# The opening of a scan-and-gate kernel: gates by token tile, a second DMA queue, and moved statistics

## The chip, the cores and the metric

The kernel runs on one core of a Trainium2 chip. The metric is the device time of one execution in microseconds. The kernel before takes 182.96 us in the median of three runs (182.48 to 183.02). Engines are named as the profile names them: PE is TensorE (PEld its weight loads), DVE is VectorE, ACT is ScalarE, POOL is GpSimd, SP is SyncE, which here only issues DMAs.

## The reference, cut to what matters

The input `x` has 2048 tokens of 448 features (bf16). It is normalised over the features, and the normalised tokens feed two branches: a diagonal complex linear recurrence over time with 448 states, and a gated feed-forward product with 1792 hidden columns. The output is `x + s * silu(branch B)`.

```python
xn = _layernorm(x, axis=-1)                       # (x - mean) / sqrt(var + 1e-5)
# branch A: recurrence
dt = exp(log_dt); Lam_bar = exp(dt * Lam); B_bar = ((Lam_bar - 1) / Lam)[:, None] * Bmat
Bu = einsum("bld,pd->blp", xn + 0j, B_bar)
for t in range(L): h = Lam_bar[None, :] * h + Bu[:, t, :]
s = 2.0 * einsum("blp,dp->bld", hseq, Cmat).real + xn * Dskip
# branch B: gated product
g = xn @ w_gate; u = xn @ w_up; z = (sigmoid(g) * u) @ w_down
return x + s * silu(z)
```

## The kernel before, in words

The 2048 tokens are cut into four chunks of 512 columns, and each chunk into four token tiles of 128 rows. A chunk is normalised by token tile, turned so that features lie on partitions (`xnT`), multiplied with the gate and up weights (14 hidden tiles of 128, `ft` 0 to 13), and with B for the recurrence (`bu`, four state tiles); the recurrence is done by VectorE with sines, cosines and a scan instruction; later come the down products (`d_ps`) and the output products (`y_ps`). 448 features are three and a half times 128: a product with `wg` or `wu` has three whole blocks (`k` = 0, 1, 2) and a half block of 64 rows in `wt` (gate tail in the upper rows of the tile, up tail in the lower). From the hidden tiles 4 and 5 on, products run as pairs of 64-row halves side by side on PE (line 514). Every engine works in the order in which the kernel writes its instructions: `keep_order` (line 60) ties each to the one before it on its engine. In the steady part a planner (`at`, `rest`, `fill`, `queue`) places VectorE's pieces beside PE's groups; it starts with `emit_line(0, ((4, 5), (6, 7), (-1, 8), (-2, 9), (-3, 10), (11, 12), (-4, 13)))`, where a positive number is a hidden tile and a negative one a state tile.

The opening is everything before that line. It is written out by hand:

- SP issues x tile 0 (line 144), x tile 1 (145), x tiles 2 and 3 (149), the gate and up weights of columns 0 to 511 (line 150, six DMAs), those of columns 512 to 1279 (line 158), and x of chunk 1 (159). ACT issues the three rows of recurrence constants (line 142). After the opening SP issues four transposing loads of B (line 294), the weights from column 1280 (line 1025), the skip row and x of chunk 2.
- Statistics of chunk 0: tiles 0, 1 and 3 by `ln_stats` on DVE (lines 216 and 217) and `ln_inv` on ACT (a logarithm and an exponential, lines 249 and 250). Tile 2 by sums and squares on ACT (lines 224 to 231), and the power on POOL (line 244).
- Each tile is normalised on DVE (line 272), turned by four PE transposes (line 286) into one of two banks `tps`, and copied to `xnT` by DVE (`ln_out`, line 289).
- PE warms up on dummy products (`warm`, line 200), then does the gate products of hidden tiles 0 to 2 on the first 256 columns (token tiles 0 and 1; `gu_wholes`, line 713), the up products on them in two parts, with the transposes of tiles 2 and 3 between, then the half blocks (`gu_half`, line 706) on the lower and the upper 256 columns, and then the whole blocks on the upper columns and hidden tile 3.
- The sine tables need, for each of the four state tiles, the angle in whole turns (`emit_whole`, ACT, line 424, rounded by a conversion to integers), its fraction and absolute fraction (`emit_frac`, `emit_abs`, DVE, lines 429 and 435), a sine and a cosine (ACT, lines 440 and 443), and a negative (`emit_neg`, DVE, line 452); POOL mirrors them later (line 455). `emit_steps`, `emit_den` are small POOL operations.
- `gu_out` and `up_copy` (lines 719 and 1000) empty the banks of hidden tiles 0 to 3 by a tanh on ACT and a halving copy on DVE. PSUM has eight banks; the eight sums of hidden tiles 0 to 3 fill them, and the group (4, 5) takes the first four that come free.
- ACT's function tables: a logarithm and exponential set is loaded at line 929; a dummy Silu at line 962 brings in the set that also has sine and tanh; the sigmoid set follows with line 752.

Of the kernel before, what the change touches and what calls it, by code (L numbers as in the profile page):

```python
# [10 lines left out]
FP32 = mybir.dt.float32  # L11
BF16 = mybir.dt.bfloat16
I32 = mybir.dt.int32
ALU = mybir.AluOpType
ACT = mybir.ActivationFunctionType

S_TOK = 2048
D = 448
F = 1792
P = 128  # L20
TC = 512
HC = TC // 2
# [10 lines left out]
GATE_K, UP_K = (0, 2, 3), (0, 1, 3)  # L33
# [3 lines left out]
MAGIC = 12582912.0  # L37
CLAMP = 1.0 - 2e-6
LN_AND_EXP = 6
SIN_SCALE = TWO_PI * CLAMP  # L40


# [29 lines left out]
def kernel(  # L72
# [17 lines left out]
    nc = tc.nc  # L90
    pe, act, dve, pool, sync = nc.tensor, nc.scalar, nc.vector, nc.gpsimd, nc.sync
    w = ctx.enter_context(tc.tile_pool(name="w", bufs=1))
    cp = ctx.enter_context(tc.tile_pool(name="cp", bufs=2))
    sp = ctx.enter_context(tc.tile_pool(name="sp", bufs=2))
# [6 lines left out]
    x_src = A_x.rearrange("b (n p) d -> p (b n) d", p=P)  # L101


    x_t = [w.tile([P, TPC, D], BF16, name=f"x{c}", tag=f"x{c}") for c in range(3)]
# [3 lines left out]
    xnT = [w.tile([P, KT, TC], BF16, name=f"xnT{c}") for c in range(3)]  # L108
    xnT.append(xnT[0])

    wg = w.tile([P, 3, F], BF16, name="wg")
    wu = w.tile([P, 3, F], BF16, name="wu")
# [11 lines left out]
    def load_w(eng, f0, f1, tails_first=False):  # L124
        def rows(mat, r0, r1):
            m = mat[r0:r1, f0:f1]
            return m.rearrange("(kt p) f -> p kt f", p=P) if r1 - r0 > P else m

        eng.dma_start(out=wg[:, 1:3, f0:f1], in_=rows(B_w_gate, 192, 448))
        eng.dma_start(out=wg[:, 0, f0:f1], in_=rows(B_w_gate, 0, 128))  # L130
        up = ((wu[:, 0:2, f0:f1], rows(B_w_up, 0, 256)), (wu[:, 2, f0:f1], rows(B_w_up, 320, 448)))
        tails = ((wt[0:64, f0:f1], rows(B_w_gate, 128, 192)), (wt[64:128, f0:f1], rows(B_w_up, 256, 320)))
        for o, i in (tails + up if tails_first else up + tails):
            eng.dma_start(out=o, in_=i)
# [7 lines left out]
        eng.dma_start(out=rows[i:i + 1, :], in_=vec.rearrange("(o p) -> o p", o=1))  # L142

    sync.dma_start(out=x_t[0][:, 0, :], in_=x_src[:, 0, :])
    sync.dma_start(out=x_t[0][:, 1, :], in_=x_src[:, 1, :])
    load_row(act, 0, A_log_dt)
    load_row(act, 1, A_Lambda_im)
    load_row(act, 2, A_Lambda_re)
# [6 lines left out]
            x_t.append(w.tile([P, TPC, D], BF16, name="x3", tag="tc_re"))  # L155
        sync.dma_start(out=x_t[c][:], in_=x_src[:, c * TPC:(c + 1) * TPC, :])

    load_w(sync, 512, 1280, True)
    load_x(1)

    ctr = {}
# [16 lines left out]
    hpi = w.tile([P, 1], FP32, name="hpi")  # L178
# [13 lines left out]
    iota_f = sp.tile([P, HC], FP32, name="iota_f", tag="ctmp")  # L192
# [5 lines left out]
    def warm(n, t=ident):  # L198
        for _ in range(n):
            pe.matmul(warm_ps[:], lhsT=t[:, 0:P], rhs=t[:, 0:P], start=True, stop=True)  # L200
# [13 lines left out]
    def ln_stats(t):  # L214
        stats = cp.tile([P, 6], FP32, name="stats")
        dve.bn_stats(out=stats[:], in_=x_t[t // TPC][:, t % TPC, :])
        dve.bn_aggr(out=mv[:, t, :], in_=stats[:])


    sums = w.tile([P, NT, 2], FP32, name="sums")  # L220

    def ln_sum(t):
        c, j = divmod(t, TPC)
        act.activation(junk[:], x_t[c][:, j, :], ACT.Copy, accum_out=sums[:, t, 0:1])

    def ln_mean(t, n):
        act.activation(mv[:, t:t + n, 0:1], sums[:, t:t + n, 0:1], ACT.Copy, scale=1.0 / D)

    def ln_square(t):
        c, j = divmod(t, TPC)  # L230
        act.activation(junk[:], x_t[c][:, j, :], ACT.Square, bias=mv[:, t, 0:1], scale=-1.0,
                       accum_out=sums[:, t, 1:2])
# [15 lines left out]
    def ln_inv(t):  # L248
        act.activation(lnv[:, t, :], mv[:, t, 1:2], ACT.Ln, bias=epsb[:])
        act.activation(rsd[:, t, :], lnv[:, t, :], ACT.Exp, scale=-0.5)  # L250

    def ln_pow_of(t, n, var, scale):
        pool.tensor_scalar(out=ve[:, t:t + n, :], in0=var, scalar1=scale, scalar2=EPS, op0=ALU.mult, op1=ALU.add)
        ln_pow(t, n)
# [30 lines left out]
        for kt in range(KT):  # L285
            pe.transpose(tps[j % 2][:, kt, :], xb[:, j, K_ROWS[kt]:K_ROWS[kt] + P], ident[:])  # L286

    def ln_out(j):
        dve.tensor_copy(out=xnT[0][:, :, j * P:(j + 1) * P], in_=tps[j % 2][:])  # L289

# [14 lines left out]
    K = {}  # L307
# [35 lines left out]
    def emit_anf():  # L343
        dve.tensor_single_scalar(out=K["anf"][:].bitcast(I32), in_=K["nf"][:].bitcast(I32), scalar=0x7FFFFFFF,
                                 op=ALU.bitwise_and)

    def emit_step_sines():
        sn, cs, nf, anf = col("sn", 2 * KT), col("cs", 2 * KT), K["nf"], K["anf"]
        act.activation(sn[:], nf[:], ACT.Sin, scale=-SIN_SCALE)
        act.activation(cs[:], anf[:], ACT.Sin, scale=-TWO_PI, bias=hpi[:])  # L350
        K.update(sn=sn, cs=cs)
# [70 lines left out]
    def emit_whole(pt):  # L422
        whole = sp.tile([P, HC], I32, name="whole", tag=("ta", "tb", "tcs", "tb")[pt])
        act.activation(whole[:], iota_f[:], ACT.Copy, scale=K["turn"][:, pt:pt + 1])
        K[pt] = whole

    def emit_frac(pt):
        f = sp.tile([P, HC], FP32, name="frac", tag="wv")
        dve.scalar_tensor_tensor(out=f[:], in0=iota_f[:], scalar=K["turn"][:, pt:pt + 1], in1=K[pt][:],
                                 op0=ALU.mult, op1=ALU.subtract)  # L430
        K[pt] = f

    def emit_abs(pt):
        af = sp.tile([P, HC], FP32, name="afrac", tag="td")
        dve.tensor_single_scalar(out=af[:].bitcast(I32), in_=K[pt][:].bitcast(I32), scalar=0x7FFFFFFF,
                                 op=ALU.bitwise_and)
        K[pt, 1] = af

    def emit_sin(pt):
        act.activation(spm[:, pt, 0, HC:TC], K[pt][:], ACT.Sin, scale=(SIN_SCALE if pt < 3 else sgp[:, 0:1]))  # L440

    def emit_cos(pt):
        act.activation(cosT[:, pt, HC:TC], K[pt, 1][:], ACT.Sin, scale=-TWO_PI, bias=hpi[:])
# [7 lines left out]
    def emit_neg(pt):  # L451
        dve.tensor_single_scalar(out=spm[:, pt, 1, HC:TC], in_=spm[:, pt, 0, HC:TC], scalar=-1.0, op=ALU.mult)
# [76 lines left out]
    class Unit:  # L529

        ft = None
# [172 lines left out]
    def gu_half(c, ft, i, t, first, n0, n1):  # L704
        p0, kt = ((0, 1), (64, 2))[i]
        pe.matmul(t[:, n0:n1], lhsT=wt[p0:p0 + 64, ft * P:(ft + 1) * P], rhs=xnT[c][p0:p0 + 64, kt, n0:n1],  # L706
                  start=first, stop=not first)

    def gu_wholes(c, ft, gt, ut, first, n0=0, n1=TC, which=(0, 1), ks=(0, 1, 2), last=True):
        f0, f1 = ft * P, (ft + 1) * P  # L710
        for t, wm, kts in [((gt, wg, GATE_K), (ut, wu, UP_K))[i] for i in which]:
            for k in ks:
                pe.matmul(t[:, n0:n1], lhsT=wm[:, k, f0:f1], rhs=xnT[c][:, kts[k], n0:n1],  # L713
                          start=(first and k == 0), stop=(not first and last and k == 2))


    def gu_out(ft, gt, ub):
# [210 lines left out]
    dummy = w.tile([P, 1], FP32, name="dummy")  # L928
# [12 lines left out]
    ln_inv(1)  # L941
    emit_dt()
    emit_angles()
    ln_sum(2)
    ln_norm(0, 0)
    ln_turn(0, 0)
    warm(2)
    ln_norm(0, 1)
    ln_turn(0, 1)
    warm(6)  # L950
    ln_out(0)
    ln_out(1)
    ln_mean(2, 1)
    ln_square(2)
    ln_pow_of(2, 1, sums[:, 2:3, 1:2], 1.0 / D)
    ln_stats(3)
    emit_whole(0)
    ln_inv(3)
    for pt in (1, 3, 2):
        emit_whole(pt)  # L960
    act.activation(K["r"][:], K["arg"][:], ACT.Exp)
    act.activation(dummy[:], hpi[:], ACT.Silu)

    emit_frac(0)
    ln_norm(0, 2)
    ln_norm(0, 3)
    for ft in range(3):
        gu_wholes(0, ft, *gus[ft], True, 0, HC, (0,))
    for ft in range(3):
        gu_wholes(0, ft, *gus[ft], True, 0, HC, (1,), (0, 1))  # L970
    ln_turn(0, 2)
    ln_out(2)
    for ft in range(3):
        gu_wholes(0, ft, *gus[ft], False, 0, HC, (1,), (2,), False)
    ln_turn(0, 3)
    ln_out(3)
    emit_abs(0)
    for pt in (1, 3, 2):
        emit_frac(pt)
        emit_abs(pt)  # L980
    gus.append((bank("g_ps"), bank("u_ps")))
    for n0 in (0, HC):
        for ft in range(3):
            for i in range(2):
                gu_half(0, ft, i, gus[ft][i], n0 > 0, n0, n0 + HC)
    for i in range(2):
        gu_half(0, 3, i, gus[3][i], True, 0, TC)
    for ft in range(4):
        gu_wholes(0, ft, *gus[ft], False, (0 if ft == 3 else HC), TC)
    emit_steps()  # L990
    emit_den()
    for pt in (0, 1, 3):
        emit_sin(pt)
        emit_cos(pt)
        if pt == 0:
            emit_neg(pt)
    ubs = [fp.tile([P, TC], BF16, name="ub") for _ in range(4)]

    def up_copy(ft):
        dve.tensor_single_scalar(out=ubs[ft][:], in_=gus[ft][1][:], scalar=0.5, op=ALU.mult)  # L1000

    for ft in range(4):
        gu_out(ft, gus[ft][0], ubs[ft])
        up_copy(ft)
        if ft == 1:
            emit_neg(1)
            emit_neg(3)
            emit_sin(2)
            emit_cos(2)
            emit_anf()  # L1010
            emit_step_sines()
    emit_neg(2)
    for pt, ft in ((0, 5), (1, 5), (2, 8), (3, 11)):
        at(0, ft, 0.0, lambda pt=pt: emit_mirror(pt))
# [7 lines left out]
    for cc in range(2):  # L1022
        for kt in (0, 2):
            emit_b(cc, kt)
    load_w(sync, 1280, F)
    sync.dma_start(out=skip[:], in_=A_Dskip.partition_broadcast(P))
    load_x(2)

# [74 lines left out]
    c = NCH - 1  # L1103
# [65 lines left out]
```

## Time and profile before

| what | value |
|---|---|
| median of the timed runs | 182.96 us (182.48 to 183.02) |
| the profiled execution's own time | 182.26 us |
| its span | 180.5 us |
| mean granted clock of PE | 0.998 |
| DMA moved | 14.27 MB, mean 79 GB/s |

The profile is one execution. Busy shares are of the span. A row of the timeline gives the start in us from the span's start, the time it covers, the engine, the line of the kernel, the operation, output and inputs with their shapes, and a count where like instructions are merged; in brackets stands the idle time before it and what ended that. A row of waits gives who waited for whom, total us, how often, and the longest. A row of the table by stretches gives busy time and count of PE, PEld, DVE, ACT and POOL, then the granted clock, the DMA share and GB/s. A DMA row's time to landing counts from the issue. Transfers of SP and of ACT have a queue each; both are served by the same 16 DMA engines that the page counts.

### The profile page before, as it was taken

The numbers are of one execution on the slowest core, as the hardware profiler recorded it, in microseconds if no ns is written. First come the engines' busy times: TensorE is split into PE (matmuls) and PEld (weight loads), VectorE is DVE, ScalarE is ACT, GpSimd is POOL, SyncE is SP. The second block draws the span as 40 slices with busy tenths as digits, with TensorE's granted clock in tenths as the row PEclk, the third lists the DMA queues.
The fourth block names the chain that finished last, engine by engine and source line by source line (L and its number), as shares of the span: only waits on it lengthen the run. The fifth ranks groups of instructions, "written<-read, shape, count | busy, mean of one in ns | idle before, by whom it ended". The sixth has DMA issues, their size and how long they took to land.

```text
span 180.5 us, 4326 instructions
## 1 busy us (share of the span) xinstructions
PE 176.2 (98%) x1637; PEld 88.2 (49%) x1637; DVE 163.4 (91%) x332; ACT 115.1 (64%) x240; POOL 23.1 (13%) x54
## 2 busy tenths in 40 slices
PE   7999999999999999999999999999999999999992
PEld 7764444445544444544544444544554444545552
DVE  4889999899999879999999999599999999499993
ACT  4999878979577887988177667047137577144100
POOL 3525668522000000003000000000000000000000
PEclk9999999999999999999999999999999999999999
DMA  5899998983442005021710020030010100011012
GB/s 150 239 292 211 245 176 168 356 185 77 99 83 53 16 4 131 5 69 36 89 31 0 4 56 2 4 102 0 4 29 0 35 0 2 4 53 51 0 32 73
DMA packets 26348, 14.27 MB, mean 79 GB/s; under 512 B 16083, under 2 KB 26070, under 8 KB 26326
## 3 DMA queue, kind: packets, MB, share of 16 engines
q1 hardware_dynamic: 26320, 13.98, 33.7%
q8 instruction: 13, 0.21, 0.5%
q14 instruction: 9, 0.07, 0.2%
q10 hardware_dynamic: 6, 0.00, 0.0%
HBM read 7.69 MB, written 1.84 MB: 53 GB/s over the span
## 4 chain that ended last, share of the span: by engine, by line
PE 97%; DVE 1%; issue 0%; DVEq 0%
PE g_ps L514 25%; PE u_ps L514 19%; PE d_ps L514 18%; PE bu L514 12%; PE y_ps L514 11%; PE d_ps L1112 6%; PE warm_ps L200 2%; PE g_ps L713 2%; PE u_ps L713 1%; PE tp_x L286 1%; DVE sg L860 0%; PE g_ps L706 0%; DVE o_l L866 0%; PE u_ps L706 0%; DVE xnT L289 0%
## 5 line engine op out<-in xcount | busy, mean ns | idle before, releaser
L514 PE MATMUL u_ps<-xnT,wu 64*128 64x512 bf16 x312 | 61.4, 376 | 0.0
L514 PE MATMUL g_ps<-xnT,wg 64*128 64x512 bf16 x312 | 53.4, 376 | 0.0
L752 ACT ACTIVATE sig<-g_ps 128x512 bf16<-128x512 f32 x52 | 29.2, 597 | 28.6 <-PE g_ps L514 28.0
L514 PE MATMUL bu<-xnT,bT 64*128 64x512 bf16 x168 | 37.4, 376 | 0.0
L514 PE MATMUL d_ps<-wd,hF 64*128 64x448 bf16 x336 | 32.3, 349 | 0.0
L514 PEld LDWEIGHTS <-wu 64*128 64x128 bf16 x312 | 22.4, 94 | 18.5
L752 ACT CAST ub<-u_ps 128x512 bf16<-128x512 f32 x52 | 29.3, 606 | 0.9 <-DVE hF L723 0.8
L514 PEld LDWEIGHTS <-wg 64*128 64x128 bf16 x312 | 18.9, 94 | 18.3 <-issue 0.4
L514 PEld LDWEIGHTS <-hF 64*128 64x128 bf16 x336 | 16.4, 94 | 15.6
L611 DVE TENSOR_TENSOR_SCAN wv<-r_col,st,ta 128x512 bf16<-128x512 f32 x18 | 22.7, 1277 | 0.2
L514 PE MATMUL y_ps<-ct,h 64*128 64x448 bf16 (+2 forms) x203 | 22.1, 343 | 0.0
L749 DVE TENSOR_TENSOR hF<-sig,ub 128x512 bf16<-128x512 bf16 x52 | 21.0, 413 | 0.4 <-ACT ub L752 0.3
L514 PEld LDWEIGHTS <-bT 64*128 64x128 bf16 x168 | 15.8, 94 | 10.0
L514 PE MATMUL g_ps<-xnT,wt 64*128 64x512 bf16 x52 | 19.6, 376 | 0.0
L514 PE MATMUL u_ps<-xnT,wt 64*128 64x512 bf16 x52 | 19.6, 376 | 0.0
L514 PEld LDWEIGHTS <-h 64*128 64x128 bf16 (+1 forms) x203 | 11.6, 95 | 9.9
L776 ACT ACTIVATE sigd<-d_ps 128x448 bf16<-128x448 f32 x12 | 6.6, 553 | 15.0 <-PE d_ps L514 15.0
L592 ACT CAST bus<-bu 128x512 bf16<-128x512 f32 x24 | 14.3, 597 | 1.7 <-PE bu L514 1.6
L514 PEld LDWEIGHTS <-wt 64*128 64x128 bf16 x104 | 9.8, 94 | 6.2
L831 DVE TENSOR_TENSOR o_t<-y_ps,xn 128x448 bf16<-128x448 f32 x12 | 6.9, 617 | 4.8 <-PE y_ps L514 4.8
L1112 PE MATMUL d_ps<-wd,hF 128*128 128x448 bf16 x56 | 10.9, 353 | 0.0
L244 POOL TENSOR_TENSOR rsd<-ve,mhalf 128x2 f32<-128x2 f32 (+2 forms) x5 | 4.6, 922 | 44.2 <-PE bu L514 44.1
(153 smaller groups left out, 239.7 us busy)
## 6 DMA issues: line engine op xcount, KB each, us to landing
wd<-in_B_w_down_dram SPq DMA_DIRECT2D x1, 1568.0 KB, 7.3
x<-in_A_x_dram SPq DMA_DIRECT2D x3, 448.0 KB, 5.0
out_dram<-o_t SPq DMA_DIRECT2D x6, 224.0 KB, 2.1
wg<-in_B_w_gate_dram SPq DMA_DIRECT2D x2, 256.0 KB, 3.6
wu<-in_B_w_up_dram SPq DMA_DIRECT2D x2, 256.0 KB, 3.7
bsw<-bus SPq DMA_DIRECT2D x4, 128.0 KB, 2.8
wsw<-wv SPq DMA_DIRECT2D x8, 64.0 KB, 1.9
c_re<-in_A_C_re_dram SPq DMA_DIRECT2D x1, 392.0 KB
```

The costliest lines, as they stand in the source:

```text
L200: pe.matmul(warm_ps[:], lhsT=t[:, 0:P], rhs=t[:, 0:P], start=True, stop=True)
L244: pool.tensor_tensor(out=rsd[:, t:t + n, :], in0=ve[:, t:t + n, :], in1=mhalf[:, 0:n, :], op=ALU.pow)
L286: pe.transpose(tps[j % 2][:, kt, :], xb[:, j, K_ROWS[kt]:K_ROWS[kt] + P], ident[:])
L514: m = pe.matmul(self.t[:, n0:n1], lhsT=lhsT, rhs=rhs, start=self.done == 1, stop=self.done == self.n)
L592: empty = [lambda cc=cc: act.copy(out=bus[:, cc, :], in_=pst[cc][:]) for cc in range(2)]
L611: dve.tensor_tensor_scan(out=T["wv"][:, cc, :], data0=rb, data1=T["ta"][:, cc, :], initial=(0.0 if c == 0 else st[pt][:, cc, :]), op0=mul, ...
L713: pe.matmul(t[:, n0:n1], lhsT=wm[:, k, f0:f1], rhs=xnT[c][:, kts[k], n0:n1], start=(first and k == 0), stop=(not first and last and k == 2))
L749: dve.tensor_tensor(out=h[:], in0=sig[:], in1=ub[:], op=ALU.mult)
L752: u.empty = [lambda: act.activation(sig[:], gt[:], ACT.Sigmoid), lambda: act.copy(out=ub[:], in_=ut[:])]
L776: act.activation(sigd[:], ds[j][:], ACT.Sigmoid)
L831: dve.tensor_tensor(out=two_runs(o[:, i, :], HD, HD), in0=two_runs(ys[c, j + 2 * i][:], HD, HD), in1=xn_runs(c, j + 2 * i), op=ALU.add)
L1112: pe.matmul(ds[j][:], lhsT=hF[c, ft][:, j * P:(j + 1) * P], rhs=wd[:, ft, :], start=ft == 0, stop=ft == FT - 1)
```

## The change

The change is in the opening only. It does the following:

- x tile 1 is issued by ACT, ahead of the three rows, and not by SP.
- The second part of the weights is columns 512 to 1151, and the third part begins at 1152, so that hidden tile 9 belongs to the third part.
- The copy of tile 1 to `xnT` is made by ACT. Four of the second batch of warm products (six) are dropped.
- Tiles 2 and 3 both get moments by DVE and roots by ACT; ACT's sums and squares of tile 2 and POOL's power go.
- The whole turns of state tiles 3 and 2 are made by POOL, in two operations each (add and subtract a large constant), in FP32.
- The dummy Silu becomes a direct load of the same table set.
- The gate products of hidden tiles 0 to 2 on the lower columns are split by token tile, the block outermost and the hidden tile inside it; block 1 comes first. Each bank is opened by its first product only, and all later products, on other columns too, go on in it.
- The first fraction moves behind the copies of tiles 2 and 3. Banks of hidden tiles 0 and 1 are emptied after the first pair of tables, those of 2 and 3 between the others.

```diff
-    sync.dma_start(out=x_t[0][:, 1, :], in_=x_src[:, 1, :])
+    act.dma_start(out=x_t[0][:, 1, :], in_=x_src[:, 1, :])
-    load_w(sync, 512, 1280, True)
+    load_w(sync, 512, 1152, True)
-    def ln_out(j):
-        dve.tensor_copy(out=xnT[0][:, :, j * P:(j + 1) * P], in_=tps[j % 2][:])
+    def ln_out(j, by_act=False):
+        (act.copy if by_act else dve.tensor_copy)(out=xnT[0][:, :, j * P:(j + 1) * P], in_=tps[j % 2][:])
+    def emit_whole_by_pool(pt):
+        whole = sp.tile([P, HC], FP32, name="whole", tag=("ta", "tb", "tcs", "tb")[pt])
+        pool.tensor_scalar(out=whole[:], in0=iota_f[:], scalar1=K["turn"][:, pt:pt + 1], scalar2=MAGIC,
+                           op0=ALU.mult, op1=ALU.add)
+        pool.tensor_single_scalar(out=whole[:], in_=whole[:], scalar=-MAGIC, op=ALU.add)
+        K[pt] = whole
+    def gu_whole(c, ft, i, t, k, n0, n1, first=False, last=False):
+        pe.matmul(t[:, n0:n1], lhsT=(wg, wu)[i][:, k, ft * P:(ft + 1) * P],
+                  rhs=xnT[c][:, (GATE_K, UP_K)[i][k], n0:n1], start=first, stop=last)
...
-    ln_sum(2)
     ln_norm(0, 0)
     ln_turn(0, 0)
     warm(2)
     ln_norm(0, 1)
     ln_turn(0, 1)
-    warm(6)
+    warm(2)
     ln_out(0)
-    ln_out(1)
-    ln_mean(2, 1)
-    ln_square(2)
-    ln_pow_of(2, 1, sums[:, 2:3, 1:2], 1.0 / D)
-    ln_stats(3)
+    ln_out(1, True)
+    for t in (2, 3):
+        ln_stats(t)
     emit_whole(0)
-    ln_inv(3)
-    for pt in (1, 3, 2):
-        emit_whole(pt)
+    for t in (2, 3):
+        ln_inv(t)
+    emit_whole(1)
+    for pt in (3, 2):
+        emit_whole_by_pool(pt)
     act.activation(K["r"][:], K["arg"][:], ACT.Exp)
-    act.activation(dummy[:], hpi[:], ACT.Silu)
-
-    emit_frac(0)
+    act.add_instruction(mybir.InstLoadActFuncSet(name=nc.get_next_instruction_name(), act_func_set_id=SILU_AND_SIN,
+                                                 ins=[], outs=[]))
     ln_norm(0, 2)
     ln_norm(0, 3)
-    for ft in range(3):
-        gu_wholes(0, ft, *gus[ft], True, 0, HC, (0,))
-    for ft in range(3):
-        gu_wholes(0, ft, *gus[ft], True, 0, HC, (1,), (0, 1))
+    def firsts(i, ks, n0, n1, first=None):
+        for k in ks:
+            for ft in range(3):
+                gu_whole(0, ft, i, gus[ft][i], k, n0, n1, k == first)
+    firsts(0, (1, 2, 0), 0, P, 1)
+    firsts(0, (1, 2, 0), P, HC)
+    firsts(1, (0, 1), 0, HC, 0)
     ln_turn(0, 2)
     ln_out(2)
-    for ft in range(3):
-        gu_wholes(0, ft, *gus[ft], False, 0, HC, (1,), (2,), False)
+    firsts(1, (2,), 0, HC)
     ln_turn(0, 3)
     ln_out(3)
-    emit_abs(0)
-    for pt in (1, 3, 2):
+    for pt in (0, 1):
         emit_frac(pt)
         emit_abs(pt)
...
-    for pt in (0, 1, 3):
-        emit_sin(pt)
-        emit_cos(pt)
-        if pt == 0:
-            emit_neg(pt)
...
+    def tables(pt):
         emit_sin(pt)
         emit_cos(pt)
+    def out(ft):
         gu_out(ft, gus[ft][0], ubs[ft])
         up_copy(ft)
+    tables(0)
+    out(0)
+    out(1)
+    emit_neg(0)
+    for pt in (3, 2):
+        emit_frac(pt)
+        emit_abs(pt)
+    tables(1)
+    tables(3)
+    emit_neg(1)
+    out(2)
+    emit_neg(3)
+    tables(2)
+    out(3)
+    emit_anf()
+    emit_step_sines()
     emit_neg(2)
...
-    load_w(sync, 1280, F)
+    load_w(sync, 1152, F)
```

## The prediction

> **What bounds the kernel now.** I read the page's busy shares and chain first, then the waits of the first 20 us, the timeline of TensorE (PE) there, and the DMA share in quarter microseconds.
>
> ```profile
> PE 176.2 (98%) x1637; PEld 88.2 (49%) x1637; DVE 163.4 (91%) x332; ACT 115.1 (64%) x240; POOL 23.1 (13%) x54
> ...
> PE 97%; DVE 1%; issue 0%; DVEq 0%
> ```
>
> PE is 98% busy and is the chain. Its windows are full from 7 us to the last stage, so a change of the opening is worth what it shifts the first line of the full stream, and nothing else.
>
> ```profile
> DVE stats L216 <- DMA x<-in_A_x_dram: 1.4, 1, 1.4
> PE g_ps L713 <- DVE xnT L289: 0.2, 1, 0.2
> PEld L713 <- DMA wu<-in_B_w_up_dram: 0.2, 1, 0.2
> ```
>
> VectorE starts when x tile 0 lands (2.77 us); PE waits a little for the copied tiles and for the first up weights.
>
> ```profile
> 6.38 1.14 PE L713 MATMUL g_ps<-xnT,wg 128*128 128x256 bf16 x9 [0.18 <-DVE xnT L289]
> 7.43 0.83 PE L713 MATMUL u_ps<-xnT,wu 128*128 128x256 bf16 x6
> 8.64 0.39 PE L286 MATMUL tp_x<-ident,xn 128*128 128x128 bf16 x4
> 9.15 0.28 PE L706 MATMUL u_ps<-xnT,wt 64*128 64x256 bf16 x1
> 9.54 0.27 PE L706 MATMUL g_ps<-xnT,wt 64*128 64x256 bf16 x1
> 10.20 0.50 PE L713 MATMUL g_ps<-xnT,wg 128*128 128x256 bf16 x3
> 13.56 0.82 PE L514 MATMUL g_ps<-xnT,wg 64*128 64x512 bf16 x6
> ```
>
> The reader is to see four marks: gates start at 6.38; the last transposes at 8.64; at 9.54 the first product on tiles 2 and 3 (the upper 256 columns); at 13.56 the full stream. From 9.54 on the list is the same before and after, so the change moves 13.56 by what it moves 9.54.
>
> ```profile
> 5.37 0.96 DVE L289 COPY xnT<-tp_x 128x512 bf16<-128x512 bf16 x2
> ...
> 8.52 0.97 DVE L289 COPY xnT<-tp_x 128x512 bf16<-128x512 bf16 x2 [0.25 <-PE tp_x L286]
> ```
>
> The second copy of the last pair ends at 9.49, 0.05 before 9.54: tile 3's copy releases the upper columns. VectorE waited 0.25 for the transposes, which stood in PE's order behind the gates and ups. So in the kernel before PE's list is the limit there; if PE gets ahead, tile 3's own chain is.
>
> **The change, part by part.** All durations are from the one profiled execution (182.26 us, span 180.5, 1.76 around it); the timed median, 182.96, is 0.70 above it.
>
> *Gates by tile.* 9 gate products of 256 columns (start to start 0.109) become 18 of 128 (four transposes take 0.22 in the chain, 0.055 each): 0.98 against 0.99, nothing. They need only tile 0's copy, 5.37 + 0.43 = 5.80, so they start at 5.85, not 6.38. The four warm-up products that go (6 to 2, about 0.06 each) lay in the wait. Opening each bank once changes flags, no instruction.
>
> *Tile 1's copy on ScalarE.* The nearest row, a ScalarE cast of 128x512 out of PSUM, is 0.61 against VectorE's 0.43. Tile 1's transposes end at 5.86, so the copy runs 5.90 to 6.50 and its gates 6.55 to 7.05. Behind it on ScalarE stand the first whole (0.49) and the roots of tiles 2 and 3.
>
> *Moments by VectorE, roots by ScalarE.* ScalarE loses tile 2's sum (0.56 + 0.19), mean (0.20) and square (0.67 + 0.19); POOL loses 0.19 + 0.58. VectorE loses a copy (0.54 apart) and gains a moments pair (0.62 + 0.18, 0.76 apart). From 5.84 the two pairs end at 7.40. ScalarE, free at 6.99, does tile 2's root to 7.5 and tile 3's (0.29, then 0.20) from 7.45 to 7.97. Tile 3's normalisation then runs 8.02 to 8.41 (8.27 before), its transposes 8.45 to 8.84 (8.64 to 9.03 before, since PE is no longer behind), its copy 8.88 to 9.31. PE's own list gets there earlier (5.85 + 18 gates 0.99 with a 0.2 wait, 9 ups 0.98, 8 transposes 0.45, lower halves 0.33, and 0.3 for tile 2) at about 9.1. So the upper columns start at 9.36: **0.18 earlier**. That, and not the 0.53 at the first gate, is the gain.
>
> *Second x tile on ScalarE's queue.* SP's issue of it (0.42, with its gap 0.47) goes, and all SP issues come 0.47 earlier: helpful to wu (waited for until 7.42) and to the first up tail (issued 4.73, landing 4.4 later, 9.13, when its product starts at 9.15). Both lie ahead of the new wait at 9.1 to 9.36 and so pay nothing more. On ScalarE the issue goes ahead of three row loads and the first table load; that load moves from 1.80 to about 2.25 and ends at 3.53, 0.12 before the first logarithm at 3.65; if the issue takes 0.6, the cover is gone and the excess is paid. The third row, issued at 1.51, goes at about 1.95; with the 2.0 that x took it lands at 3.95, against PE's use at 3.86: 0 to 0.1; I take 0.
>
> ```profile
> 1.75:2.00 0.25, 0.25 (x5) 0.25 (x3) 0.00 (x0) 0.20 (x1) 0.25 (x1) 1.00 0.77 186
> 2.00:2.25 0.25, 0.25 (x6) 0.25 (x4) 0.00 (x0) 0.25 (x1) 0.07 (x1) 1.00 0.71 226
> 2.25:2.50 0.25, 0.25 (x5) 0.25 (x4) 0.00 (x0) 0.25 (x1) 0.00 (x0) 1.00 0.88 226
> ```
>
> The last two columns are the DMA share and GB/s. Tile 0 is 115 KB, about 0.5 us at these rates, and tile 1 followed it 0.45 later. Issued at the same moment, both share engines that are 0.7 to 0.9 busy: tile 0 lands between 0 (no sharing) and 0.45 later (both done in 1.0). The nearest row is the spare share of a quarter, which lets about half be hidden: I take **+0.2**. Everything on tile 0 shifts with it; tile 1 gains nothing, since its moments follow tile 0's at 3.53 without a wait.
> [...]
>
> *Two wholes on POOL.* Four POOL operations of 256 columns (nearest row: the cast of iota_f, 0.40) from 5.9 to about 7.6; the ten small steps behind them (7.49 to 10.17 before) end near 10.5, with the sine of 14.21 as cover. But VectorE's normalisations at 7.5 to 8.4 now run beside them:
>
> ```profile
> 21.90 0.67 POOL L457 COPY spm<-spm 128x510 bf16<-128x510 bf16 x1
> 22.02 0.69 DVE L272 TENSOR_SCALAR xn<-x,mv,rsd 128x512 bf16<-128x512 bf16 x1
> 23.30 0.41 DVE L272 TENSOR_SCALAR xn<-x,mv,rsd 128x512 bf16<-128x512 bf16 x1
> ```
>
> The same operation took 0.69 beside a POOL copy and 0.41 without. Cost 0 to 0.4 (one POOL operation); most of POOL's four are over by then: **+0.1**.
> [...]
>
> *Order of the tables and drains.* The dummy (0.20) goes. The first fraction (0.48) moves from 7.02, ahead of the normalisations, behind tile 3's copy; so VectorE, without a pause from 12.5 on, reaches its first hF product 0.4 to 0.7 later than 15.38, and ScalarE, whose last sine waits for VectorE's fourth up copy, starts the sigmoid table at about 16.2, not 15.58. Cover: the group at 19.62 takes banks that ScalarE freed by 17.97 and 18.93, of which the last is wanted only at about 20.4; 0.65 later leaves 0.9. ScalarE's up copy that waited for hF (21.30) frees a bank wanted at about 23.4. POOL's mirrors come after 15.5 and wait for signs done by 14.5. So 0, and PE pays only beyond 0.9.
>
> *Smaller second part.* ft 9's columns move to the third part. Fewer bytes are ahead of x1 and the B transposes; the price is in the second rival.
>
> Sum: -0.18 + 0.2 + 0.1 = +0.12. Profiled 182.38; on the median 182.96 + 0.12 = **183.1 us**, no change that shows: 0.3% (0.55 us) is about what a measurement of this kernel can tell.
>
> **The rivals.** (1) *Faster: PE's list sets the pace.* If tile 0 lands as before, POOL does not touch the normalisations and tile 3's copy ends by 9.0, PE starts at 5.85 and needs 6.55 us of products and transposes, with 0.3 of changes between array shapes and 0.3 of waits: 13.0 instead of 13.56, 182.4. For it: the kernel before lost 0.19 for a tail, 0.18 for a copy, and those go. Against: the chain of tile 3 above has no slack to give 0.3 more.
> (2) *Slower: ft 9's last tail is late.* The up tail of the third part was issued at 19.84; ft 10 wanted it at 26.75, ft 9 wants it at 23.72, where PE loads ft 9's tail now. Tails landed 3.5 to 5.5 after issue (median 4.9). With SP 0.47 ahead: 22.9 to 24.9. PE stops from a landing time of 4.35 on; at 5.0 it costs 0.65, with the sum 183.7; at 5.5 184.2. Against: fewer bytes ahead should bring the issue forward by more than 0.47 and lighten the queue.
> (3) *Slower: the opening's unknowns at their upper ends.* -0.18 + 0.45 + 0.4 = +0.67, 183.6. It decides where tile 3's copy ends after 10.0.
> (4) *ScalarE's late sigmoid stops the group at 19.6.* From 1.5 us of lateness on; I see 0.65.
>
> **How the numbers follow.** Forecast (within 0.55 us, 182.4 to 183.5) 0.42; rival 1 0.25, all of it counted faster; rival 2 0.16, rival 3 0.11, rival 4 and the like 0.06, together 0.33 slower. The range reaches into rival 1 to 182.0 and over most of rivals 2 and 3 to 184.0; what is outside is under 2 in 10. The forecast alone would be 182.7 to 183.5 (-0.18 to +0.5).
>
> **What would show it.** First gate at 5.9 to 6.1; wait of the first moments for x 1.4 to 1.6; the normalisations of tiles 2 and 3 0.37 each or longer; the first 64-row product on the upper columns at 9.36 to 9.9, after a pause of PE; first line of the full stream 13.4 to 13.9; no PE pause at 23.7. I am wrong if that line stands before 13.1 or a pause appears after it.

## The result: slower by 0.6%

The changed kernel takes 183.86 us in the median of 14 executions (182.38 to 184.82), the kernel before 182.55 us in the median of 14 taken beside them (182.26 to 184.34). The recorded ratio is 1.0064, with a 95% interval of 1.0042 to 1.0086 (the quotient of the two medians is 1.0072). That is past the 0.3% that such a measurement can tell from no change.

The executions of the changed kernel fall into two groups: four at 182.38 to 182.96, and ten at 183.60 to 184.82. Of the kernel before, one in these 14 lies above 183.5, and none in the sets of 26, 23 and 23 measured beside the experiments. What differs between the groups is the subject of what follows. The profiled execution of the changed kernel, 184.27 us with a span of 182.5, belongs to the upper group; it stands 2.01 us above the profiled execution of before.

The marks of the prediction, in the timeline of PE of the changed kernel:

```profile
4.27 0.22 PE L206 MATMUL tp_v<-ident,rows 3*128 3x3 bf16 x3 [0.34 <-DMA rows<-in_A_Lambda_re_dram]
...
6.63 2.13 PE L718 MATMUL g_ps<-xnT,wg 128*128 128x128 bf16 x18
8.55 1.49 PE L718 MATMUL u_ps<-xnT,wu 128*128 128x256 bf16 x6
...
10.58 0.39 PE L287 MATMUL tp_x<-ident,xn 128*128 128x128 bf16 x4
...
11.48 0.27 PE L714 MATMUL g_ps<-xnT,wt 64*128 64x256 bf16 x1
...
15.50 0.82 PE L522 MATMUL g_ps<-xnT,wg 64*128 64x512 bf16 x6
```

The full stream begins at 15.50 instead of 13.56, which is 1.94 of the 2.01 us, so the opening holds nearly all of the loss. It splits at the marks. The first gate is 0.25 late (6.63 for 6.38). From the first gate to the first up product PE takes 1.92 instead of 1.05: the 18 products of 128 columns go by at 0.107 us each, not at the 0.055 that the prediction used (+0.87). From there to tile 3's transposes it takes 2.03 instead of 1.21, with the ups of 256 columns at 0.213 instead of 0.109 each (+0.82). From tile 3's transposes to the full stream it takes 4.92 in both. PE waits for no other engine or transfer in those 3.95 us, and each product takes about twice its time of before. It ran at half pace: the record of the clock has full pace from 10.22 on.

The chain of the changed kernel, its first pieces (start, us, what), shows where the lateness at the first gate comes from:

```profile
0.72 0.40 ACTq L146
...
1.15 0.53 ACTq L143
...
1.71 0.23 ACTq L143
...
1.97 2.17 DMA rows<-in_A_Lambda_re_dram
...
4.27 0.22 PE tp_v L206 x3
```

Before, the chain went over PE's own warm-up products from 0.97 on, and the turn of the rows followed them without a wait. The kernel before, for this reading and the next:

```profile
0.97 2.95 PE L200 MATMUL warm_ps<-junk 128*128 128x128 bf16 x26 [0.97 <-DVE junk L177]
...
2.77 0.63 DVE L216 BATCH_NORM_STATS2 stats<-x 128x6 f32<-128x448 bf16 x1 [1.35 <-DMA x<-in_A_x_dram]
...
3.86 0.23 PE L205 MATMUL tp_v<-ident,rows 3*128 3x3 bf16 x3
...
7.57 0.70 DVE L272 TENSOR_SCALAR xn<-x,mv,rsd 128x448 bf16<-128x448 bf16 x2
```

Now it starts with ACT's issue of x tile 1 (line 146), ahead of the three rows (line 143). The last row goes out at 1.97 and not at 1.51, needs 2.17 to land, and PE turns the rows at 4.27 and not at 3.86.

VectorE's timeline in the changed kernel, for the other late input:

```profile
3.40 0.63 DVE L217 BATCH_NORM_STATS2 stats<-x 128x6 f32<-128x448 bf16 x1 [1.99 <-DMA x<-in_A_x_dram]
...
8.11 1.01 DVE L273 TENSOR_SCALAR xn<-x,mv,rsd 128x448 bf16<-128x448 bf16 x2 [0.25 <-ACT rsd L251]
10.45 0.97 DVE L290 COPY xnT<-tp_x 128x512 bf16<-128x512 bf16 x2 [1.33 <-PE tp_x L287]
```

Tile 0's moments start at 3.40, 0.63 later than before. The two normalisations of tiles 2 and 3 take 1.01 together, where two took 0.70. And VectorE waits 1.33 for the transposes: in this execution tile 3's chain is not what holds PE, PE's own pace is.

### The profile page after: what moved, and what is told of

The parts are those of the page before. It is cut to its first block, busy times and chain, and to the rows that moved or that the text cites. A ratio compares the mean times of both kernels' runs of the same rounds, so it can differ in the third digit from the quotient of the medians.

```text
span 182.5 us, 4333 instructions
## 1 busy us (share of the span) xinstructions
PE 177.9 (97%) x1641; PEld 125.9 (69%) x1642; DVE 165.2 (91%) x333; ACT 113.7 (62%) x235; POOL 24.8 (14%) x56
## 4 chain that ended last, share of the span: by engine, by line
PE 95%; DMA 1%; DVE 1%; ACTq 1%; issue 0%; DVEq 0%
PE g_ps L522 23%; PE u_ps L522 20%; PE d_ps L522 17%; PE bu L522 12%; PE y_ps L522 11%; PE d_ps L1129 6%; PE g_ps L718 2%; PE u_ps L718 2%; DMA rows<-in_A_Lambda_re_dram 1%; PE tp_x L287 1%; PE warm_ps L201 1%; DVE sg L865 0%; ACTq L143 0%; PE g_ps L714 0%; DVE o_l L871 0%
## 5 line engine op out<-in xcount | busy, mean ns | idle before, releaser
L522 PE MATMUL u_ps<-xnT,wu 64*128 64x512 bf16 x312 | 59.5, 376 | 0.0
L522 PE MATMUL g_ps<-xnT,wg 64*128 64x512 bf16 x312 | 55.3, 376 | 0.0
L522 PEld LDWEIGHTS <-wu 64*128 64x128 bf16 x312 | 26.2, 94 | 11.0
L522 PEld LDWEIGHTS <-wg 64*128 64x128 bf16 x312 | 24.5, 94 | 11.0 <-issue 0.4
L522 PEld LDWEIGHTS <-hF 64*128 64x128 bf16 x336 | 26.2, 94 | 5.8
L754 DVE TENSOR_TENSOR hF<-sig,ub 128x512 bf16<-128x512 bf16 x52 | 21.5, 423 | 0.4 <-ACT ub L757 0.3
L522 PEld LDWEIGHTS <-h 64*128 64x128 bf16 (+1 forms) x203 | 16.5, 95 | 5.0
L245 POOL TENSOR_TENSOR rsd<-ve,mhalf 128x2 f32<-128x2 f32 (+1 forms) x4 | 4.9, 1220 | 45.1 <-PE bu L522 44.6
```

The costliest lines, as they stand in the source:

```text
L245: pool.tensor_tensor(out=rsd[:, t:t + n, :], in0=ve[:, t:t + n, :], in1=mhalf[:, 0:n, :], op=ALU.pow)
L522: m = pe.matmul(self.t[:, n0:n1], lhsT=lhsT, rhs=rhs, start=self.done == 1, stop=self.done == self.n)
L754: dve.tensor_tensor(out=h[:], in0=sig[:], in1=ub[:], op=ALU.mult)
```

## The experiments

The theories when the first runs were chosen: (A) PE's clock is held at half because PE had too little to do early on, through late data or fewer warm products; (B) the data is late and PE only passes the lateness on; (C) POOL's wholes and VectorE's longer list delay tile 3. All medians are of the timed executions; "above 183.5" counts those of the upper group. The kernel before, measured beside each set of runs, had a median of 182.40 to 182.55. The ratios are the recorded ones and not quotients of the medians.

| run | median us | ratio to before (95%) | above 183.5 | full stream in its profile |
|---|---|---|---|---|
| changed kernel | 183.86 | 1.0064 (1.0042 to 1.0086) | 10 of 14 | 15.50 |
| x1_back_on_sp | 182.68 | 1.0030 (1.0005 to 1.0054) | 3 of 12 | 13.66 |
| x1_on_act_in_before | 183.57 | 1.0065 (1.0044 to 1.0087) | 7 of 11 | 16.04 |
| less_warm_in_before | 184.34 | 1.0101 (1.0083 to 1.0119) | 6 of 6 | 16.21 |
| more_warm_in_after | 183.04 | 1.0042 (1.0018 to 1.0066) | 2 of 10 | 13.78 |
| two_warm_in_before | 182.44 | 0.9999 (0.9990 to 1.0007) | 0 of 11 | 13.52 |
| six_warm_in_after | 184.14 | 1.0087 (1.0069 to 1.0105) | 5 of 6 | 15.28 |
| more_warm_part_1280 | 184.12 | 1.0073 (1.0045 to 1.0101) | 5 of 6 | 13.62 |
| x1_on_act_after_rows | 185.10 | 1.0144 (1.0122 to 1.0167) | 6 of 6 | 17.32 |
| x1_sp_wholes_on_act | 182.44 | 1.0005 (0.9989 to 1.0022) | 1 of 12 | 13.93 |
| all_four_undone | 182.61 | 1.0006 (0.9998 to 1.0015) | 0 of 11 | 13.65 |
| roots_first | 182.18 | 0.9991 (0.9982 to 1.0000) | 0 of 11 | 13.41 |

**The x tile's queue, undone and alone.** First, the changed kernel with x tile 1 back on SP:

```diff
-    act.dma_start(out=x_t[0][:, 1, :], in_=x_src[:, 1, :])
+    sync.dma_start(out=x_t[0][:, 1, :], in_=x_src[:, 1, :])
```

> The changed kernel with x tile 1 issued by SP again; all else as changed. In the changed kernel's trace x tile 0 landed 2.7 us after its issue (2.0 before), PE stood idle or on tiny products from 3.9 to 4.6 us, and then ran its gates at 0.107 us for 128 columns, twice the 0.055 of the transposes that follow 10 us. Theory A (half pace: too little work on PE in its first microseconds keeps it at half pace some 4.6 us longer) and theory B (the data are late and PE hands the lateness on): both expect tile 0's moments back at 2.8, gates at full pace from about 6 us on, the full stream at 13.4 to 13.9, and 182.3 to 183.0 us against 182.55 before. Theory C (POOL's wholes beside the normalisations, and VectorE's longer list, are the loss): x tile 0 has little to do with it, and the time stays near 183.6.

Then the reverse edit of the same line in the kernel before, and nothing else:

```diff
-    sync.dma_start(out=x_t[0][:, 1, :], in_=x_src[:, 1, :])
+    act.dma_start(out=x_t[0][:, 1, :], in_=x_src[:, 1, :])
```

> The kernel before with x tile 1 issued by ACT ahead of the rows, nothing else changed. Theory A: tile 0 lands near 3.4 and PE has less work early, but four warm-up products more than the changed kernel; some executions lose the early full pace and cost 1.3 to 1.9 more, so a median of 182.9 to 184.5 and a wide spread between executions. Theory B: all executions later by about tile 0's lateness, 0.6: 183.1 to 183.3 with a narrow spread. Theory C: no change, 182.4 to 182.8.

The edit alone costs the kernel before as much as the whole change does (1.0065 beside 1.0064), and undoing it takes much of the loss away: the median falls by 1.18 us, the ratio, which three of twelve executions above 183.5 still raise, from 1.0064 to 1.0030. The timeline of PE with x tile 1 back on SP:

```profile
6.06 1.38 PE L718 MATMUL g_ps<-xnT,wg 128*128 128x128 bf16 x18
7.53 0.83 PE L718 MATMUL u_ps<-xnT,wu 128*128 128x256 bf16 x6
...
13.66 0.82 PE L522 MATMUL g_ps<-xnT,wg 64*128 64x512 bf16 x6
```

The first gate stands inside the 5.9 to 6.1 that the prediction gave. The pace becomes full during the gates (18 in 1.38, where the changed kernel took 2.13), and the full stream is 0.10 later than before.

With the line moved in the kernel before, the timeline of PE and two stretches of the span (PE's granted clock is the third column from the end):

```profile
5.01 0.21 PE L205 MATMUL tp_v<-ident,rows 3*128 3x3 bf16 x3 [1.11 <-DMA rows<-in_A_Lambda_re_dram]
...
7.40 2.08 PE L713 MATMUL g_ps<-xnT,wg 128*128 128x256 bf16 x9 [0.18 <-DVE xnT L289]
```

```profile
3.75:7.15 3.40, 1.89 (x28) 1.51 (x27) 2.30 (x8) 2.15 (x10) 0.71 (x3) 1.00 0.89 255
7.20:10.50 3.30, 3.12 (x16) 2.16 (x15) 2.04 (x6) 3.21 (x10) 2.25 (x10) 0.50 0.92 254
```

Here the clock column shows it. In the stretch in which PE waited 1.11 for the row it was busy 1.89 of 3.40 us, and in the next 3.41 us the clock was granted at 0.50. The record of the clock has full pace from 3.75, half pace from 7.16 and full pace again from 10.58. So the lateness of the data costs twice in this run: once as a wait, and then as half pace for the stretch behind it (nine gates in 2.08 instead of 1.14). That is (A) by way of late data; by (B) alone the products would have kept their 0.055 and 0.109.

**When is the pace lifted?** With x tile 1 moved alone, the changes on record lie 3.41 and 3.42 us apart (3.75, 7.16, 10.58). The first change on record stands at another place of the opening in each of three profiles: 3.75 there, 5.59 in the kernel before, 10.22 in the changed one. Stretches of that length, counted back from the first change, for the kernel before (full from 5.59 on) and the changed one (full from 10.22 on):

```profile
2.18:5.59 3.41, 3.41 (x36) 3.03 (x34) 2.40 (x7) 2.64 (x9) 0.41 (x2) 1.00 0.91 253
```

```profile
0.00:3.40 3.40, 2.43 (x23) 2.43 (x24) 0.43 (x11) 1.13 (x1) 1.40 (x8) 1.00 0.48 137
3.40:6.81 3.41, 3.06 (x29) 2.37 (x28) 3.02 (x8) 1.45 (x8) 0.91 (x4) 1.00 0.83 252
```

PE was busy all of the stretch ahead of its full pace in the kernel before, and 2.43 and 3.06 of the two after which half pace went on in the changed one; the third, 6.81 to 10.22, was busy throughout. (The clock column says 1.00 ahead of the first change on record, though the products go at half pace; there it is no evidence.) The busy time is a modelled one, and not a clean measure: with x tile 1 moved alone, the pace was full behind a stretch with 2.78 busy (0.33 to 3.75). Counted in columns streamed (an estimate: each row's columns of the timeline, spread over its time), the stretch ahead of full pace had about 3600 in the kernel before and 3160 with x tile 1 moved alone; the two after which half pace went on had about 2730 and 2960 in the changed kernel. That the work in such a stretch decides the pace is a reading of these rows and not shown apart.

The paces themselves are in the rows: 0.107 and 0.055 us for 128 columns. The same gap at 4 us may spoil the pace in one execution and not in another, which would make two groups out of one program; execution by execution that is not shown, since only one of each series was profiled.

**Warm products.** Does PE's pace hang on the dummy products that the change removed, or on the gaps? The kernel before without its thirteen warm products behind the rows:

```diff
-    warm(5)
...
-    warm(2)
...
-    warm(6)
```

> The kernel before without the 13 warm-up products that follow the turning of the rows (the groups of 5, 2 and 6); x tile 1 stays on SP, tile 0 lands as before. This prices the half pace by itself. Theory A: PE stays at half pace to about 9 or 10 us in nearly all executions, gates of 256 columns take 0.213 each, and the time is 183.6 to 184.6. Theory B and C: the products filled waits only, 182.4 to 182.8.

Here the data is on time (moments from 2.76), all executions lie above 183.5, and the full stream starts at 16.21; the record has full pace from 12.24 on. So less work for PE, with x and the rows on time, is enough for half pace; the price is +1.9 in the median. The profiled execution also waited 0.74 for gate weights at its first gate, so its 16.21 is not the price of the missing products alone; whether the other five executions had that wait isn't shown.

The change removed only four, all behind tile 1's transposes. That edit alone in the kernel before, and undone in the changed one:

```diff
     ln_turn(0, 1)
-    warm(6)
+    warm(2)
```

> The kernel before, with two warm products instead of six behind the transposes of tile 1 (one of the edits of the change, alone; x tile 1 stays on SP). If the fewer warm products are a cause by themselves: several executions in ten at 183.6 or above, median up by 0.3 us or more. If they only matter where the data is late (the prediction counted them as lying in a wait): 182.4 to 182.7 median, at most one execution in ten above 183.5, full stream at 13.5 to 13.7.

> The changed kernel with six warm products instead of two behind the transposes of tile 1 (that one edit undone; x tile 1 stays on ScalarE's queue). If the late data is the main cause: the executions still lie mostly at 183.6 and above, as in the changed kernel (10 of 14), median 183.7 to 184.6; in an execution at full pace the full stream stands at 13.7 to 13.9 and the third part's late weights add up to 0.7. If the fewer warm products are the main cause: mostly 182.4 to 183.2, median below 183.1.

Two instead of six cost nothing where the data is on time (0.9999): PE's wait ahead of the first gate grew from 0.18 to 0.40, so the four products were lying in a wait there. Six again do not help where the data is late (184.14): at half pace they hold the first gate up by 0.50 (7.13 for 6.63), and the record has full pace only from 9.25 on. That leaves the gap ahead of them. The attempt to fill it, with five more products in the changed kernel:

```diff
-    warm(26, junk)
+    warm(29, junk)
...
-    warm(5)
+    warm(7)
```

> The changed kernel with five more warm-up products, placed where PE was idle: three on the junk tile before the rows are turned (26 to 29), two after (5 to 7). Tile 0 stays late, near 3.4. Theory A: PE reaches full pace by 6 to 7 us in nearly all executions, the gates run at 0.055 for 128 columns, and the time falls to 182.6 to 183.2 with a spread under 0.8. Theory B and C: nothing to gain, 183.6 to 184 as the changed kernel.

The profiled execution ran at full pace from 5.50 on, with 18 gates in 1.26 and a full stream at 13.78, 0.22 behind before; and yet it took 183.26. The missing 0.7 us lies behind the opening, in the timeline of PE's weight loads:

```profile
23.93 0.09 PEld L522 LDWEIGHTS <-wu 64*128 64x128 bf16 x1 [0.55 <-DMA wu<-in_B_w_up_dram]
...
24.83 0.09 PEld L522 LDWEIGHTS <-wt 64*128 64x128 bf16 x1 [0.43 <-DMA wt<-in_B_w_up_dram]
```

This is the prediction's second rival, to the place: ft 9's weights in the third part, the up tail issued at 20.22, its weight load released at 24.83. The changed kernel itself shows no such pause. It comes there 1.94 later, but its tail also went out earlier, at 19.18, and which of the two spares it isn't shown: with x tile 1 back on SP the tail went out at 19.42, PE loaded it on time at 23.82, and no pause stands there either. So the price hangs on when SP gets to the third part, which differs between the profiles by over 1 us. To test the place, the second part's size was put back as well:

```diff
-    load_w(sync, 512, 1152, True)
+    load_w(sync, 512, 1280, True)
...
-    load_w(sync, 1152, F)
+    load_w(sync, 1280, F)
```

> The changed kernel with the five extra warm products and with the second weight part at its size of before (up to column 1280). The run with the extra warm products alone had the full stream at 13.78 and yet 183.26 us, with pauses of PE of 0.22 and 0.24 us at 23.9 and 24.8 in front of ft 9's up products, whose weights came with the third part. Theory (rival 2 of the prediction, hidden in the changed kernel because PE came there 1.9 us late): with ft 9 in the second part the pauses are gone, the full stream still starts at 13.7 to 13.9, and the profiled time is 182.5 to 182.7, 0.6 to 0.7 lower. If something else made the pauses (VectorE's late hF, a bank), they stay and the time is 183.1 to 183.3.

In the profiled execution the pauses are gone, the full stream stands at 13.62 and the time is 182.39: 0.87 less, of which 0.16 is the opening and the rest the pauses. But the other five executions lie at 184.01 to 184.31, while of the run above, with the same warm products, two of ten lie above 183.5. The profile shows only the sixth, so half pace is the likely reading of the five and not a shown one. The two series ran on different chips and differ in the second part's size, and which of these parts them isn't shown; what they do show is that five more dummy products are no sure cure.

**Where in the queue?** If the rows' lateness is the trouble, x tile 1 could stay on ACT's queue behind them:

```diff
-    act.dma_start(out=x_t[0][:, 1, :], in_=x_src[:, 1, :])
     load_row(act, 0, A_log_dt)
     load_row(act, 1, A_Lambda_im)
     load_row(act, 2, A_Lambda_re)
+    act.dma_start(out=x_t[0][:, 1, :], in_=x_src[:, 1, :])
```

> The changed kernel with x tile 1 on ScalarE's queue, but issued behind the three rows (about 1.5 to 2.0 us instead of 0.72). Theory (tile 0 and the rows are late because tile 1's transfer shares the DMA engines with them and stands ahead of the rows; PE then idles and its clock is held at half): tile 0 lands 2.0 us after its issue, its moments start at 2.8, PE's turn of the rows at 3.9 without a wait, PE at full pace at the first gate, SP's later issues 0.3 to 0.5 earlier than before the change; tile 1's moments wait for x until about 3.9 to 4.0 (3.58 otherwise), so its gates are 0.3 later; full stream 13.6 to 14.0, 182.6 to 183.0 us, with few executions above 183.5. Rival (a second issuer by itself is the cost, or the fewer warm products by themselves): half pace again until about 10, full stream 15.4 to 16, 183.9 to 184.7.

A miss for both sides. VectorE's timeline in that run:

```profile
2.79 0.63 DVE L217 BATCH_NORM_STATS2 stats<-x 128x6 f32<-128x448 bf16 x1 [1.37 <-DMA x<-in_A_x_dram]
...
5.60 0.63 DVE L217 BATCH_NORM_STATS2 stats<-x 128x6 f32<-128x448 bf16 x1 [1.97 <-DMA x<-in_A_x_dram]
```

Tile 0 is on time again (moments from 2.79), as with x tile 1 back on SP (2.82): what delayed it was tile 1's issue at the same moment. But tile 1, issued at 1.82, lands 3.8 us later and not 2.0. SP has issued the tiles 2 and 3 and gate weights (1.18 to 2.62) in the meantime; that these held it up is the likely cause and not shown apart. VectorE takes tile 1's moments ahead of tile 0's normalisation in its order, so PE idles 1.72 at its first transposes, goes at half pace once more (18 gates in 2.13), and the median is 185.10.

**POOL's wholes.** x tile 1 on SP, and all four wholes on ScalarE:

```diff
-        emit_whole_by_pool(pt)
+        emit_whole(pt)
```

> The changed kernel with x tile 1 back on SP's queue, and with all four wholes on ScalarE (none on POOL). To be set against the run with x tile 1 on SP alone: 182.69 us, the two normalisations 1.00 us, the first upper columns at 9.65, the full stream at 13.66. Theory C (POOL's wholes slow VectorE's normalisations, and through tile 3's chain PE): the two normalisations take 0.70 to 0.75 again, the upper columns start 0.1 to 0.25 earlier (9.4 to 9.55), the full stream at 13.4 to 13.55, undisturbed executions 182.45 to 182.6. [...] If PE's own list is what orders the last transposes (8.74) by now, the normalisations get shorter and the time moves by less than 0.1.

The two normalisations with x tile 1 on SP and the wholes on POOL, and then with the wholes on ACT:

```profile
7.53 1.00 DVE L273 TENSOR_SCALAR xn<-x,mv,rsd 128x448 bf16<-128x448 bf16 x2 [0.26 <-ACT rsd L251]
```

```profile
7.31 0.40 DVE L273 TENSOR_SCALAR xn<-x,mv,rsd 128x448 bf16<-128x448 bf16 x1
7.88 0.40 DVE L273 TENSOR_SCALAR xn<-x,mv,rsd 128x448 bf16<-128x448 bf16 x1 [0.17 <-ACT rsd L251]
```

Theory C holds in its effect: the two normalisations take 0.80 instead of 1.00. Its price is small and not set apart from the noise: the median moves from 182.68 to 182.44, the ratio from 1.0030 to 1.0005, the intervals overlap, and the two series ran on different chips. This profile can't be used for the full stream, since PE waited 0.55 for gate weights in it.

**What is left of the change.** All four undone: x tile 1 on SP, wholes on ScalarE, six warm products, second part to column 1279 (the diffs above, together, in the changed kernel).

> The changed kernel with x tile 1 on SP, the wholes on ScalarE, six warm products instead of two, and the second weight part at its old size. What is left of the change: gates by tile in banks opened once, tile 1's copy by ScalarE, moments of tiles 2 and 3 by VectorE with roots by ScalarE, and the order of the tables. If the losses are the four things undone, it is no slower than the kernel before: full stream at 13.4 to 13.55, 182.3 to 182.6, nearly no execution above 183.5. If one of the parts that are left costs time as well, it stays at 182.7 to 183.0. If a gain of the size that rival 1 of the prediction promised is there, it shows 182.1 or less.

It is the kernel before to within 0.2% (1.0006, 0.9998 to 1.0015): the gates by tile, tile 1's copy on ScalarE, the moved moments and the new order of the tables together cost nothing, and gain nothing; one by one they were not tried. The gates start at 6.28 in this profile (6.38 before), but the upper columns at 9.63 (9.54 before), right behind the end of tile 3's copy at 9.57: PE gives the time back at tile 3's chain, which the prediction named, though it saw the upper columns 0.18 earlier than before and not 0.09 later. Hence the last run, which shortens that chain: the first whole behind the roots, and the transposes one group of up products earlier.

```diff
-    emit_whole(0)
     for t in (2, 3):
         ln_inv(t)
-    emit_whole(1)
-    for pt in (3, 2):
+    for pt in (0, 1, 3, 2):
         emit_whole(pt)
...
-    firsts(1, (0, 1), 0, HC, 0)
+    firsts(1, (0,), 0, HC, 0)
     ln_turn(0, 2)
     ln_out(2)
-    firsts(1, (2,), 0, HC)
+    firsts(1, (1,), 0, HC)
     ln_turn(0, 3)
     ln_out(3)
+    firsts(1, (2,), 0, HC)
```

> The version with the four things undone, and two steps moved: ScalarE's first whole behind the roots of tiles 2 and 3, and tile 2's and tile 3's transposes each one group of three up products earlier in PE's list. If tile 3's chain sets the start of the upper columns, as the run with the four things undone suggests (roots behind the whole, normalisations at 7.59 and 8.14, copies until 9.57, upper columns at 9.6): normalisations at about 7.4 and 8.0, copies until 9.3, upper columns at 9.3 to 9.4, full stream at 13.3 to 13.45 instead of 13.65, 182.2 to 182.4 us median, faster than before by 0.05 to 0.2%. If the rest of the opening (PE's own products and the weights) is as tight, it stays at 182.5 to 182.6.

Its timeline of PE, from the first gate on:

```profile
5.95 1.44 PE L718 MATMUL g_ps<-xnT,wg 128*128 128x128 bf16 x18
...
8.42 0.39 PE L287 MATMUL tp_x<-ident,xn 128*128 128x128 bf16 x4
...
13.41 0.82 PE L522 MATMUL g_ps<-xnT,wg 64*128 64x512 bf16 x6
```

Tile 3's transposes stand at 8.42 instead of 8.73, the full stream at 13.41, and the median is 182.18 against 182.40: 0.9991, with an interval that just reaches 1. It is the fastest of the versions run. Tile 3's copy ends at 9.27, and the first upper product at 9.41 follows the lower ones without a pause, so PE's own list is the limit there and no longer the chain. The full stream comes 0.15 earlier than before; rival 1 of the prediction had seen 0.56 there.

## Where the prediction was right and where it was wrong, step by step

It named no change as likeliest and 183.1 us; 183.86 is inside its range and on the side that it gave 0.33. That it lies inside is luck. The sum was +0.12, and +1.31 was measured. The range reached up to 184.0 for rivals 2 and 3, of which the first did not occur here and the second holds only a part of what happened, and it was counted from the 182.96 of three runs, where 14 give 182.55; counted from there its upper end would be 183.6. By its own steps:

- *Second x tile on ScalarE's queue: +0.2, between 0 and 0.45.* This is the step that failed, in three ways. Tile 0 landed 2.7 after its issue instead of 2.0, and its moments began 0.63 later: outside the range, which stopped at full sharing between the two tiles. The rows, where "I take 0" stood, came 0.41 later at PE: the prediction had seen that the third row's cover was thin (3.95 against 3.86) and then assumed for it the 2.0 that x tile 0 took before. It took 2.17 in the changed kernel, and with the line moved alone PE waited 1.11. And the lateness was priced at one to one. The upper end of the range, 0.45, was nearer the measured 0.63 than the 0.2 taken, but even with it the sum would have been +0.37, not +1.3.
- *All SP issues 0.47 earlier.* Not so in the profile of the changed kernel: the first part's up weights went out at 3.22 instead of 3.13, behind a gap at SP from 2.64. With x tile 1 moved alone they went out at 3.46, and with five more warm products at 3.42, so there the second queue did not even save SP's time. With x tile 1 behind the rows they went out at 2.66, as the prediction had it; what held SP in these three isn't shown. The third part did come earlier (16.23 instead of 17.19).
- *A price that is not in the sum at all: PE's pace.* Every product was costed at the full-pace duration of the kernel before. None of the four rivals has a change of pace in it. In the profile of before the evidence was there, unread: the first 26 warm-up products of 128 columns cover 2.95 us, 0.113 each, and tile 2's four transposes of 128 columns 0.22, 0.055 each. This missing term is 1.69 of the 1.94 us (0.87 + 0.82).
- *The dropped warm products lay in a wait: 0.* Right for those four with the data on time, shown by the run with two of them; it would be wrong for all thirteen (+1.9).
- *Gates by tile: nothing but an earlier start, 5.85.* Right in kind: 6.06 with x tile 1 on SP, 5.95 in the last run, and the gain is not kept.
- *Tile 3's chain, upper columns 0.18 earlier.* Not met, even at full pace: 9.64 with x tile 1 on SP, where the sum had 9.36. There the normalisations end at 8.53 (8.41 in the sum) and the two copies run back to back from 8.62 to 9.59 (9.31 in the sum), because tile 2's copy already starts late behind PE's list. With ScalarE's first whole behind the roots and the transposes moved, the full stream came 0.15 earlier than before.
- *Wholes on POOL: +0.1, between 0 and 0.4.* Right in place: two normalisations in 1.00 instead of 0.80 with ScalarE's wholes; the about 0.2 us in the medians are within the noise of the two series. The reason given for the small size was wrong: POOL's four operations were not over by 7.6 but ran, with x tile 1 on SP, from 6.03 to 8.85 (0.48 and 0.87 each, not 0.40), beside both normalisations.
- *Tables, drains, late sigmoid: 0.* Right. Neither the changed kernel's profile nor the one with x tile 1 on SP, which comes there on time, has a wait of PE for a bank between 15 and 30 us.
- *Rival 2, ft 9's late weights, 183.7 to 184.2.* It can come true and did not in the changed kernel: 183.26 where the tail went out at 20.22, a wait of 0.25 for it where it went out at 19.81 (wholes on ScalarE), and no pause with PE on time where it went out at 19.42 (x tile 1 on SP, 182.69).
- *Rival 3, the opening's unknowns at their upper ends, 183.6.* Right in its sign and in the x tile; the rows and the pace are not in it, and its sum of +0.67 is half of what was measured.

Two things stay open. With x tile 1 on SP and POOL's wholes three of twelve executions still lay above 183.5, and one of twelve with ScalarE's wholes; none of them was profiled. And it was not tried what a version does that keeps PE busy without a gap while x tile 1 stays on ACT's queue.

## What to carry to other kernels

Read the duration of like products at several places of the opening before costing anything there: here they took twice as long early on (0.107 us for 128 columns instead of 0.055), and a wait of 0.34 us went with a loss of 1.69 in pace. A second issuing queue was no gain here: with what it moved forward came a delay of what was first (0.63 at tile 0's moments) and of the small loads behind it on its own queue (0.41 at the turn of the rows), so look up who uses those small loads first. When an edit makes a stage late, ask what would stop the engine further on if the stage were on time: the late weights showed only in profiles whose opening was back on time.

## What the runs showed of the hardware

- With x tile 1 moved alone in the kernel before, PE was busy 1.89 of the 3.40 us from 3.75 on, with 1.11 as the longest wait, and the following 3.41 us had the clock at 0.50. In the kernel before the record is full from 5.59 to 179.67 and at 0.50 from there to the end of its span at 180.5, where PE had no more work (0.00 busy from 179.70 to 180.40); in the changed kernel it is full from 10.22 to the end of its span.
- The same program gave 182.4 and 184.8 us in one series on one core, with nothing changed but the execution.
- 112 KB of x tile 1 landed 2.5 us after its issue by ACT at 0.72, 2.1 after SP's issue at 1.17, and 3.8 after ACT's issue at 1.82, after SP had issued the tiles 2 and 3 (224 KB) and 256 KB of gate weights.
